# Windowed attention with a Mish MLP on one core: two key blocks merged by a predicated copy before the exponential

## Chip, cores and metric

The kernel runs on one core of one Trainium2 chip. The metric is the device time of one execution in microseconds (us); less is better. TensorE (PE), VectorE (DVE), ScalarE (ACT), GpSimd (POOL) and SyncE (SP, which issues the DMAs) each work through a queue of their own in order, and wait for one another through semaphores.

## What is computed

```python
def _attn_ref(q, k, v):                       # (8, 8, 576, 64) each
    scores = q @ k^T / sqrt(64)
    rel = pos[:, None] - pos[None, :]
    bias = slope[h] * -abs(rel)
    mask = (rel >= 0) & (rel < 128)
    attn = softmax(where(mask, scores + bias, -1e9))
    return attn @ v
def _moe_ref(x, w_in, w_out):                 # x (4608, 512), d_ff 2048
    h = x @ w_in
    g = h * tanh(softplus(h))                 # Mish
    return g @ w_out
```

A query sees itself and the 127 keys before it. With queries in blocks of 128, row r of a block sees the keys n <= r of its own block and the keys n > r of the block before: 128 keys in all, one for each column n.

## The kernel before

**Work.** There are 8 batches of 8 heads; heads go in pairs (4 pairs, `p`), and each pair has three units: `unit(b, p, 0)` (half 0: query blocks 0 and 1), `unit(b, p, 1)` (half 1: blocks 2 and 3) and `last_unit(b, p)` (the 64 queries that are left of 576; both heads in one tile). A unit is a list of steps: `scores` (PE, into a PSUM tile `s` of two banks, of which there are two), `peak` (DVE adds the bias table `nb`, finds the row's extreme `mx` and writes the scores to `pz`), `exps` (ACT, the sum goes to `sm`), `fold`, `scale`, `weights` (PE transposes the attention weights back into `s`, DVE copies them out), `values` (PE, into `o`), and `split_hi`/`split_lo` (ACT and DVE write the result as a high and a low float32r part, `x`).

**Two key blocks.** `peak` and `exps` work on 256 columns for each query block (128 for block 0, which has no block before it): the older key block and the own one, masked by the bias table. In batches 1 to 7 `fold` then adds the two halves of `pz` on GpSimd, so that 128 columns are left, `scale` multiplies by the reciprocal sums on DVE (lines 241-244), `weights` makes four transposes, and one DVE product with `masks` spreads them over two key blocks again (lines 263-268). In batch 0 nothing is folded: GpSimd scales 256 columns a block (lines 232-240), PE makes 6 or 8 transposes and DVE copies them (lines 249-259). The last queries' scores go into the unused columns of half 0's `s` tile in batches 1 to 7 (line 328), into a tile `w` in batch 0.

**MLP.** `first(c, j)` makes `h` (PE, 24 products of 512 columns, three for each of the four pairs' x and each half of `j`), 8 of them a batch; `h` shares the two buffers of `s`, and ACT's Mish empties one. `parts` splits g (ACT `gs`, GpSimd `gs`); `second` makes `po` in groups of six products. Weights arrive as 64-bit values and pass `sign_w` (ACT), `bits_w` (two DVE instructions, `ti`/`to`), `high_w` (ACT, `si`/`so`) and `low_w` (DVE).

**What sets the order.** Every instruction is recorded in program order (all appear under line 30). The program order is a sort of steps by hand-written times: batch 0 and the weights from `START`, `UNIT`, `X0`, `signs` and `bits` (lines 511-535); then, for each batch c, its `first` steps, followed by its `second` steps with the attention of batch c+1 laid between them at `4 * s + 0.8` (line 558). The numbers beside the steps (lines 303-315, 390-396) are those times.

Of the kernel before, what the change touches and what calls it, by code (L numbers as in the profile page):

```python
# [16 lines left out]
P = 128  # L17
# [20 lines left out]
def attention_mish_mlp(  # L38
# [69 lines left out]
    nl = const.tile([P, NP, 192], BF16, tag="nl", name="nl")  # L108
# [11 lines left out]
    make_upper_triangular(nc, masks[:, 1, :])  # L120
    xs = dram.tile([NCC, P, CH], F32, tag="xs", name="xs")
# [48 lines left out]
    def unit(b, p, half):  # L170
# [10 lines left out]
        def scores():  # L181
            qk = qkv[(b, p)]
            if b == 0 and (2 * p + half) % 3 == 2:
                s_ = [ps.tile([P, 512], F32, tag=f"po{i}", name=f"s{name}_{i}") for i in range(2)]
            else:
                t = ps.tile([P, 2, 512], F32, tag="s", name=f"s{name}", bufs=2)
                s_ = [t[:, i, :] for i in range(2)]
                if half == 0:
                    qkv[("s", b, p)] = t[:, :, :96]
            st["s"] = s_  # L190
            q0 = 0 if half == 0 else 832
            for a, j in enumerate(blocks):
                n = 256 if j else P
                for i in range(2):
                    pe.matmul(
                        s_[i][:, 256 * (a + 1) - n : 256 * (a + 1)], lhsT=qk[HEAD[i], q0 + a * P : q0 + (a + 1) * P],
                        rhs=qk[HEAD[i], 256 + (j + 1) * P - n : 256 + (j + 1) * P], start=True, stop=True,
                    )

        def peak(a):  # L200
            if a == 0:
                st["mx"] = at.tile([P, 4], F32, tag="mx", name=f"mx{name}")
                st["sm"] = at.tile([P, 4], F32, tag="sm", name=f"sm{name}")
                st["pz"] = at.tile([P, 4, 256], F32, tag="pz", name=f"pz{name}")
            mx, pz = st["mx"], st["pz"]
            n = 256 if blocks[a] else P
            for c in (a, a + 2):
                dve.tensor_tensor_reduce(
                    out=pz[:, c, :n], in0=st["s"][c // 2][:, 256 * (a + 1) - n : 256 * (a + 1)],
                    in1=nb[:, p, c // 2, 256 - n :], scale=-SCALE, scalar=3.0e38,  # L210
                    op0=ALU.add, op1=ALU.min, accum_out=mx[:, c : c + 1],
                )
# [10 lines left out]
        def fold():  # L223
            sm, pz = st["sm"], st["pz"]
            if b:
                two = pz if half else pz[:, 1:4:2]
                pool.tensor_tensor(out=two[:, :, :P], in0=two[:, :, :P], in1=two[:, :, P:], op=ALU.add)
            dve.tensor_scalar(out=sm, in0=sm, scalar1=1e-9, scalar2=None, op0=ALU.add)
            dve.reciprocal(sm, sm)

        def scale():
            if b == 0:
                for a, j in enumerate(blocks):
                    n = 256 if j else P
                    pool.tensor_tensor(
                        out=st["pz"][:, a::2, :n], in0=st["pz"][:, a::2, :n],
                        in1=st["sm"][:, a::2].rearrange("p (c n) -> p c n", n=1).to_broadcast([P, 2, n]),
                        op=ALU.mult,
                    )
                return  # L240
            dve.tensor_tensor(
                out=st["pz"][:, :, :P], in0=st["pz"][:, :, :P],
                in1=st["sm"].rearrange("p (c n) -> p c n", n=1).to_broadcast([P, 4, P]), op=ALU.mult,
            )

        def weights():
            pz = st["pz"]

            if b == 0:
                pf = st["pf"] = ff.tile([P, 2, 512], F32, tag="g", name=f"pf{name}", bufs=3)  # L250
                first = 0 if half else P
                for i in range(2):
                    for a, j in enumerate(blocks):
                        for u in range(2 if j else 1):
                            d = 256 * a + P * u if j else P
                            pe.transpose(st["s"][i][:, d : d + P], pz[:, 2 * i + a, u * P : (u + 1) * P], ident)
                for i in range(2):
                    dve.tensor_copy(pf[:, i, first:], st["s"][i][:, first:])
                return
# [3 lines left out]
            dve.tensor_tensor(  # L263
                out=pz.rearrange("p c (u n) -> p u c n", u=2),
# [4 lines left out]

# [33 lines left out]
        if b == 0:  # L303
            return [
                (0, scores), (0.1, lambda: peak(0)), (0.1, lambda: exps(0)), (0.15, lambda: peak(1)),
                (0.15, lambda: exps(1)), (0.5, fold), (0.55, scale),
                (1.6, weights), (2.25, values), (2.38, split_hi),
                (2.9 if p + 1 < NP else 2.4, split_lo),
# [3 lines left out]
            (0, scores), (0.02 + t, lambda: peak(0)), (0.025 + t, lambda: peak(1)),  # L312
            (0.026 + 27 * t, lambda: exps(0)), (0.026 + 27 * t, lambda: exps(1)), (0.27 + 33 * t, fold),
# [3 lines left out]
    def last_unit(b, p):  # L317
# [4 lines left out]
        def scores():  # L322
            qk = qkv[(b, p)]
            if b == 0:
                st["t"] = ps.tile([P, 512], F32, tag="w", name=f"pt{name}")
                st["s"] = st["t"][:, 256:448].rearrange("p (a n) -> p a n", a=2)
            else:
                st["s"] = qkv[("s", b, p)]
            for i in range(2):
                pe.matmul(  # L330
                    st["s"][:, i, :], lhsT=qk[:, 1152:1280], rhs=qk[:, 640 + 96 * i : 736 + 96 * i],
                    start=True, stop=True,
                )

        def peak():
            mx = st["mx"] = at.tile([P, 1], F32, tag="mxl", name=f"mx{name}")
            sm = st["sm"] = at.tile([P, 1], F32, tag="sml", name=f"sm{name}")
            pz = st["pz"] = at.tile([P, 192], F32, tag="pzl", name=f"pz{name}")
            dve.tensor_tensor_reduce(
                out=pz.rearrange("p (a n) -> p a n", a=2), in0=st["s"],  # L340
                in1=nl[:, p, :].rearrange("p (a n) -> p a n", a=2), scale=-SCALE, scalar=3.0e38,
# [3 lines left out]
        def exps():  # L345
            act.activation(st["pz"], st["pz"], AF.Exp, bias=st["mx"], scale=-1.0, accum_out=st["sm"])

        def fold():
            sm, pz = st["sm"], st["pz"]
            dve.tensor_scalar(out=sm, in0=sm, scalar1=1e-9, scalar2=None, op0=ALU.add)  # L350
            dve.reciprocal(sm, sm)
            if b == 0:
                pool.tensor_scalar(out=pz, in0=pz, scalar1=sm, scalar2=None, op0=ALU.mult)
                return
            dve.tensor_tensor(out=pz[:, :64], in0=pz[:, :64], in1=pz[:, P:], op=ALU.add)
            dve.tensor_scalar(out=pz[:, :P], in0=pz[:, :P], scalar1=sm, scalar2=None, op0=ALU.mult)
# [20 lines left out]
        def values():  # L377
            va = qkv[("v", b, p)]
            o = st["t"][:, P : P + LEFT]
            for n in range(2):  # L380
                k = 64 if n and b == 0 else P
                for i in range(2):
                    pe.matmul(
                        o[HEAD[i]], lhsT=va[:k, 3 + n, HEAD[i]], rhs=st["pf"][:k, n, i, :],
                        start=(n == 0), stop=(n == 1), skip_group_check=True,
                    )
            xo = at.tile([P, LEFT], F32, tag="xo", name=f"xo{name}", bufs=4)
# [6 lines left out]
        if b == 0:  # L394
            return [(0.28, scores), (0.3, peak), (0.3, exps), (1.3, fold), (1.65, weights), (2.12, values)]
        return [
            (0.01, scores), (0.04, peak), (0.31, exps), (0.5, fold), (1.54, weights), (1.995, values),
# [33 lines left out]
    def first(c, j):  # L431
        h = ps.tile([P, 2, CH], F32, tag="s", name=f"h{c}_{j}", bufs=2)
        split = NCC - 1 if c and j == 0 else NCC
# [78 lines left out]
    X0 = START + 9.45 * UNIT  # L512
# [133 lines left out]
```

## Time and profile before

| what | value |
|---|---|
| median of 3 runs | 1023.83 us (1023.41 to 1024.63) |
| the profiled execution's own time | 1023.82 us |
| its span in the trace | 1022.1 us |
| mean granted TensorE clock | 0.992 of full speed |
| busy shares PE, DVE, ACT, POOL | 96%, 42%, 37%, 26% |
| chain that ended last | PE 76%, DVE 12%, ACT 9%, issue 2% |

The busy share of PE says how much of the span some matmul was under way; what counts are the gaps, and the releaser named beside each. Times in the rows are microseconds from the span's start.

### The profile page before, as it was taken

To read this page: it belongs to the slowest core of one execution; us is meant where nothing else is said; L and a number is where in the kernel's file an instruction comes from. 1 tells how busy PE (TensorE), PEld (TensorE's weight loads), DVE (VectorE), ACT (ScalarE), POOL (GpSimd) and SP (SyncE) were. 2 spreads that over 40 slices of the span, in tenths; PEclk is the share of its full clock that TensorE was granted. 3 is DMA by queue.
4 is the path that set the end of the run, shared out by engine and by line. 5 is a ranking of instruction groups with operands and counts; after the bars stand their busy time and mean duration, and the time that the engine had idled before them with its cause. 6 is when DMAs were issued, how large, how long until landed. Compare 5 with 4: busy or idle time off the path is not lost.

```text
span 1022.1 us, 13726 instructions
## 1 busy us (share of the span) xinstructions
PE 979.1 (96%) x5308; PEld 790.9 (77%) x5308; DVE 425.3 (42%) x1118; ACT 377.8 (37%) x898; POOL 261.0 (26%) x230
## 2 busy tenths in 40 slices
PE   7799889999999999999999999999999999999998
PEld 4588668877788778877788778877887778888886
DVE  5797874046700763057502671077404770010000
ACT  4875533244323433245324342253324432331221
POOL 4310431033301531045103340144104330241043
PEclk8999999999999999999999999999999999999999
DMA  9930112003110121012200121021200201010001
GB/s 370 419 134 27 41 61 75 1 26 98 44 35 15 52 78 59 1 39 89 75 1 27 63 80 35 1 66 62 75 1 26 76 4 41 1 42 21 1 6 36
DMA packets 23392, 61.37 MB, mean 60 GB/s; under 512 B 6688, under 2 KB 7840, under 8 KB 21280
## 3 DMA queue, kind: packets, MB, share of 16 engines
q1 hardware_dynamic: 22096, 59.78, 17.2%
q8 instruction: 42, 0.69, 0.3%
q10 hardware_dynamic: 1232, 0.72, 0.2%
q14 instruction: 22, 0.18, 0.1%
HBM read 50.00 MB, written 10.49 MB: 59 GB/s over the span
## 4 chain that ended last, share of the span: by engine, by line
PE 76%; DVE 12%; ACT 9%; issue 2%; DMA 0%; POOL 0%; DVEq 0%; POOLq 0%; ACTq 0%
PE h L30 38%; PE po L30 22%; PE s L30 9%; ACT pz L30 7%; PE o L30 5%; DVE pz L30 5%; DVE pz_1l L30 1%; DVE pz_2l L30 1%; DVE pz_0l L30 1%; ACT gs L30 1%; DVE sm L30 1%; PE pt_0l L30 0%; PE pt_1l L30 0%; DVE pf L30 0%; PE pt_3l L30 0%
## 5 line engine op out<-in xcount | busy, mean ns | idle before, releaser
L30 PE MATMUL po<-so,gs 128*128 128x512 f32 x1728 | 411.8, 394 | 1.5 <-ACT gs L30 1.1
L30 PE MATMUL h<-x,si 128*128 128x512 f32 x1728 | 394.5, 390 | 1.2 <-DVE si L30 1.2
L30 PEld LDWEIGHTS h<-x,si 128*128 128x128 f32 x1728 | 323.7, 188 | 69.2 <-DVE si L30 1.7
L30 PEld LDWEIGHTS po<-so,gs 128*128 128x128 f32 x1728 | 321.7, 189 | 67.8 <-ACT gs L30 1.5
L30 POOL TENSOR_TENSOR gs<-g,gs 128x512 fp32r<-128x512 f32 x144 | 186.6, 1300 | 568.4 <-ACT gs L30 545.5
L30 DVE CUSTOM_DVE_ANT_0 pz<-s,nb 128x256 f32<-128x256 f32 (+1 forms) x256 | 82.6, 386 | 310.7 <-PE s L30 310.0
L30 ACT ACTIVATE g<-h 128x1024 f32<-128x1024 f32 x72 | 74.0, 1028 | 273.1 <-PE h L30 273.1
L30 ACT ACTIVATE pz<-pz,mx 128x256 f32<-128x256 f32 (+1 forms) x256 | 119.9, 470 | 70.4 <-DVE mx L30 70.4
L30 ACT ACTIVATE gs<-g 128x512 fp32r<-128x512 f32 x144 | 88.7, 624 | 127.1 <-PE po L30 127.1
L30 POOL TENSOR_TENSOR pz<-pz 128x256 f32<-128x256 f32 (+1 forms) x56 | 57.4, 1024 | 158.1 <-ACT pz L30 158.1
L30 PE MATMUL s<-qk 64*128 64x256 f32 (+2 forms) x624 | 77.8, 360 | 3.8 <-DMA qk<-in_qk_dram 3.8
L30 DVE TENSOR_TENSOR pz<-pz,sm 128x512 f32<-128x512 f32 x56 | 78.9, 1409 | 5.8
L30 PEld LDWEIGHTS s<-qk 64*128 64x128 f32 (+1 forms) x624 | 57.1, 192 | 21.2 <-issue 12.8
L30 DVE TENSOR_TENSOR pz<-s,masks 128x1024 f32<-128x1024 f32 x56 | 65.7, 1212 | 8.0 <-PE s L30 7.9
L30 PE MATMUL s<-ident,pz 128*128 128x128 f32 x280 | 43.6, 289 | 25.1 <-DVE pz L30 23.9
L30 PEld LDWEIGHTS s<-ident,pz 128*128 128x128 f32 x280 | 33.9, 148 | 34.9 <-issue 29.2
L30 DVE COPY ob<-po 128x512 f32<-128x512 f32 x18 | 12.3, 682 | 114.3 <-PE po L30 114.3
L30 ACT ACTIVATE x<-o 128x512 fp32r<-128x512 f32 x32 | 19.0, 594 | 95.0 <-PE o L30 95.0
L30 PE MATMUL o<-pz,va 128*64 128x128 f32 (+1 forms) x560 | 48.7, 320 | 0.0
L30 ACT ACTIVATION_READ_ACCUMULATOR pz<-pz,mx 128x1 f32 x256 | 48.0, 187 | 0.0
L30 PEld LDWEIGHTS o<-pz,va 128*64 128x64 f32 x560 | 33.9, 136 | 18.0 <-issue 7.4
L30 ACT ACTIVATE ob<-po 128x512 f32<-128x512 f32 x18 | 10.7, 596 | 51.4 <-PE po L30 51.4
(120 smaller groups left out, 388.6 us busy)
## 6 DMA issues: line engine op xcount, KB each, us to landing
qk<-in_qk_dram SPq DMA_DIRECT2D x31, 640.0 KB, 4.4
va<-in_v_dram SPq DMA_DIRECT2D x28, 320.0 KB, 3.3
wi<-in_moe_w_in_dram SPq DMA_DIRECT2D x8, 1024.0 KB, 14.3
wo<-in_moe_w_out_dram SPq DMA_DIRECT2D x8, 1024.0 KB, 20.4
out_dram<-ob SPq DMA_DIRECT2D x32, 256.0 KB, 2.0
qk<-in_v_dram SPq DMA_DIRECT2D x4, 320.0 KB, 6.3
xr<-xs SPq DMA_DIRECT2D x4, 256.0 KB, 2.8
out_dram<-ob SPq DMA_DIRECT2D x8, 128.0 KB, 2.3
```

The source lines that it names most:

```text
L30: ins = method(*args, **kwargs)
```

## The change

- The two key blocks are merged ahead of the exponential. A mask `older` (GpSimd builds it at the start) drives a DVE `copy_predicated` that overwrites, in PSUM, the own block's score by the older block's where n > r. `peak` then has 128 columns for every block, with a bias table to match, `exps` has 128 columns, and the fold is gone. The last queries get the same.
- `scale` moves to GpSimd for all batches (for the last queries in batch 0 alone); `sums` keeps the two small DVE instructions of `fold`.
- Batch 0 uses the way of the other batches: four transposes and one product with `masks`.
- The last queries' scores always get a tile of their own (`w`, in batch 0 `po1` for odd pairs); `values` is split, with `keep` writing the result out.
- The written times of batch 0 and of the weights are new; `first(0, 0)` takes the last pair's x behind the other three; the first Mish is placed at 3.2 instead of 0.3 behind its slot.

```diff
-    nl = const.tile([P, NP, 192], BF16, tag="nl", name="nl")
+    nl = const.tile([P, NP, P], BF16, tag="nl", name="nl")
...
+    older = const.tile([P, 192], BF16, tag="older", name="older")
+    make_upper_triangular(nc, older[:, :P], diag=False)
+    for i in range(2):
+        make_lower_triangular(nc, older[i * D : (i + 1) * D, P:])
+    older = older.bitcast(mybir.dt.uint16)
...
-            if b == 0 and (2 * p + half) % 3 == 2:
-                s_ = [ps.tile([P, 512], F32, tag=f"po{i}", name=f"s{name}_{i}") for i in range(2)]
...
+            t = ps.tile([P, 2, 512], F32, tag="s", name=f"s{name}", bufs=2)
+            st["s"] = [t[:, i, :] for i in range(2)]
+            st["all"] = t.rearrange("p i (c u n) -> p (i c) u n", u=2, n=P)
...
+        def peak():
...
+            v = st["all"] if half else st["all"][:, 1::2]
+            n = v.shape[1]
+            dve.copy_predicated(
+                v[:, :, 1], older[:, :P].rearrange("p (c n) -> p c n", c=1).to_broadcast([P, n, P]), v[:, :, 0]
+            )
+            for a, j in enumerate(blocks):
+                for i in range(2):
+                    dve.tensor_tensor_reduce(
+                        out=pz[:, 2 * i + a, :P], in0=st["s"][i][:, 256 * a + P : 256 * a + 256],
...
+            for c in (0, 2, 1, 3):
                 act.activation(
-                    pz[:, c, :n], pz[:, c, :n], AF.Exp, bias=mx[:, c : c + 1], scale=-1.0,
+                    st["pz"][:, c, :P], st["pz"][:, c, :P], AF.Exp, bias=st["mx"][:, c : c + 1], scale=-1.0,
...
-                pool.tensor_tensor(out=two[:, :, :P], in0=two[:, :, :P], in1=two[:, :, P:], op=ALU.add)
...
-            dve.tensor_tensor(
+            pool.tensor_tensor(
                 out=st["pz"][:, :, :P], in0=st["pz"][:, :, :P],
                 in1=st["sm"].rearrange("p (c n) -> p c n", n=1).to_broadcast([P, 4, P]), op=ALU.mult,
...
+            pf = st["pf"] = ff.tile([P, 4, 256], F32, tag="g", name=f"pf{name}", bufs=3) if b == 0 else pz
...
-                (0, scores), (0.1, lambda: peak(0)), (0.1, lambda: exps(0)), (0.15, lambda: peak(1)),
-                (0.15, lambda: exps(1)), (0.5, fold), (0.55, scale),
-                (1.6, weights), (2.25, values), (2.38, split_hi),
-                (2.9 if p + 1 < NP else 2.4, split_lo),
+                (-0.38 if p or half else 0, scores), (0.1, peak), (0.15, exps), (0.6, sums), (0.62, scale),
+                (1.3, weights), (1.75, values), (2.2 if p + 1 < NP else 1.85, split_hi),
+                ({NP - 2: 3.4, NP - 1: 1.98}.get(p, 2.62), split_lo),
...
-                st["s"] = qkv[("s", b, p)]
...
+            t = st["t"] = ps.tile([P, 512], F32, tag="po1" if b == 0 and p % 2 else "w", name=f"pt{name}")
...
+            dve.copy_predicated(older_[:, :64], older[:, P:], newer)
...
-    X0 = START + 9.45 * UNIT
+    X0 = START + 9.0 * UNIT
...
+    signs = [START + UNIT * t for t in (3.25, 4.25, 5.25, 6.25, 7.2, 7.5, 7.72, 8.2)]
+    signs += [X0 + t for t in (0.9, 1.9, 2.9, 3.9, 5.9, 8.4)]
...
-        steps.append((t + SLOT + 0.3, lambda j=j: mish[j]()))
+        steps.append((t + SLOT + (0.3 if j else 3.2), lambda j=j: mish[j]()))
```

**How the order moves.** In the rows below a tile's name ends in pair, half and a number, or in pair and `l` for the last queries.

DVE in batch 1, pair 2, from the last queries' scores to the masks, before:

```order
L30 RECIPROCAL sm_2_0_1199<-sm_2_0_1199 128x4
L30 TENSOR_TENSOR pz_2_0_1200<-pz_2_0_1200,sm_2_0_1199 128x4x128
L30 TENSOR_SCALAR sm_2l<-sm_2l 128x1
L30 RECIPROCAL sm_2l<-sm_2l 128x1
L30 TENSOR_TENSOR pz_2l<-pz_2l 128x64
L30 TENSOR_SCALAR pz_2l<-pz_2l,sm_2l 128x128
L30 TENSOR_SCALAR sm_2_1_1210<-sm_2_1_1210 128x4
L30 RECIPROCAL sm_2_1_1210<-sm_2_1_1210 128x4
L30 TENSOR_TENSOR pz_2_1_1211<-pz_2_1_1211,sm_2_1_1210 128x4x128
L30 TENSOR_TENSOR pz_2_0_1200<-s_2_0_1181,masks 128x2x4x128
L30 TENSOR_TENSOR pz_2_1_1211<-s_2_1_1186,masks 128x2x4x128
L30 TENSOR_TENSOR pf_2l<-pt_2l,masks 128x256
```

The same stretch with the change:

```order
L30 RECIPROCAL sm_2_0_1177<-sm_2_0_1177 128x4
L30 TENSOR_SCALAR sm_2l<-sm_2l 128x1
L30 RECIPROCAL sm_2l<-sm_2l 128x1
L30 TENSOR_SCALAR pz_2l<-pz_2l,sm_2l 128x128
L30 TENSOR_SCALAR sm_2_1_1205<-sm_2_1_1205 128x4
L30 RECIPROCAL sm_2_1_1205<-sm_2_1_1205 128x4
L30 TENSOR_TENSOR pz_2_0_1171<-s_2_0_1152,masks 128x2x4x128
L30 TENSOR_TENSOR pz_2_1_1183<-s_2_1_1157,masks 128x2x4x128
L30 TENSOR_TENSOR pf_2l<-pt_2l,masks 128x256
```

The two 512-column products by `sm` and the 64-column sum are gone from DVE; the small instructions on the sums stand close together.

GpSimd in the same pair, before:

```order
L30 TENSOR_TENSOR gs_1_2_1153<-g_1_659,gs_1_2_1153 128x512
L30 TENSOR_TENSOR pz_2_0_1200<-pz_2_0_1200 128x2x128
L30 TENSOR_TENSOR gs_1_3_1230<-g_1_659,gs_1_3_1230 128x512
L30 TENSOR_TENSOR pz_2_1_1211<-pz_2_1_1211 128x4x128
L30 TENSOR_TENSOR gs_1_4_1259<-g_2_739,gs_1_4_1259 128x512
```

With the change:

```order
L30 TENSOR_TENSOR gs_1_2_1124<-g_1_627,gs_1_2_1124 128x512
L30 TENSOR_TENSOR gs_1_3_1202<-g_1_627,gs_1_3_1202 128x512
L30 TENSOR_TENSOR pz_2_0_1171<-pz_2_0_1171,sm_2_0_1177 128x4x128
L30 TENSOR_TENSOR pz_2_1_1183<-pz_2_1_1183,sm_2_1_1205 128x4x128
L30 TENSOR_TENSOR gs_1_4_1231<-g_2_704,gs_1_4_1231 128x512
```

The two folds became two scalings, and `gs` of part 3 stands ahead of both instead of between them.

ACT around the first Mish (`g` from `h`), before:

```order
L30 ACTIVATE si_554<-ti_541 128x1024
L30 ACTIVATE x_3_556<-o_3_521 128x512
L30 ACTIVATE wo_127<-wo_127 128x1024
L30 ACTIVATE wo_129<-wo_129 128x1024
L30 ACTIVATE wo_131<-wo_131 128x1024
L30 ACTIVATE wo_133<-wo_133 128x1024
L30 ACTIVATE wo_135<-wo_135 128x1024
L30 ACTIVATE si_594<-ti_587 128x1024
L30 ACT_TABLE_LOAD
L30 ACTIVATE g_0_584<-h_0_559 128x1024
L30 ACTIVATE si_626<-ti_596 128x1024
L30 ACTIVATE si_632<-ti_628 128x1024
```

With the change:

```order
L30 ACTIVATE x_3_519<-o_3_492 128x512
L30 ACTIVATE si_525<-ti_522 128x1024
L30 ACTIVATE wo_134<-wo_134 128x1024
L30 ACTIVATE wo_136<-wo_136 128x1024
L30 ACTIVATE wo_138<-wo_138 128x1024
L30 ACTIVATE wo_140<-wo_140 128x1024
L30 ACTIVATE wo_142<-wo_142 128x1024
L30 ACTIVATE si_589<-ti_560 128x1024
L30 ACTIVATE wo_144<-wo_144 128x1024
L30 ACT_TABLE_LOAD
L30 ACTIVATE g_0_553<-h_0_528 128x1024
L30 ACTIVATE si_597<-ti_591 128x1024
```

One pass on `wo` more stands behind `si` of the second weight block and ahead of the first Mish, and the last pair's `x` now stands ahead of that `si`.

## Rows read from the trace of the kernel before

**Rows 1.** The waits of PE over the span (us in total, times, longest)

```profile
PE s L30 <- DVE pz L30: 23.9, 21, 3.1
```

**Rows 2.** Timeline of PE in batch 2, pair 0: start, duration, instruction, [idle before]

```profile
225.81 0.60 PE L30 MATMUL s<-ident,pz 128*128 128x128 f32 x4
227.38 0.63 PE L30 MATMUL s<-ident,pz 128*128 128x128 f32 x4 [0.97 <-DVE pz L30]
...
230.80 1.74 PE L30 MATMUL o<-pz,va 128*64 128x256 f32 x20
...
232.70 2.40 PE L30 MATMUL s<-qk 64*128 64x128 f32 x20
```

**Rows 3.** Timeline of DVE in the same stretch

```profile
217.78 0.29 DVE L30 CUSTOM_DVE_ANT_0 pz<-s,nb 128x128 f32<-128x128 f32 x1 [46.34 <-PE s L30]
...
217.99 0.28 DVE L30 CUSTOM_DVE_ANT_0 pz<-s,nb 128x128 f32<-128x128 f32 x1
...
225.58 1.66 DVE L30 TENSOR_TENSOR pz<-pz,sm 128x512 f32<-128x512 f32 x1
227.16 2.34 DVE L30 TENSOR_TENSOR pz<-s,masks 128x1024 f32<-128x1024 f32 x2
...
233.22 0.69 DVE L30 TENSOR_TENSOR x<-o,x 128x512 fp32r<-128x512 f32 x1 [0.17 <-ACT x L30]
```

**Rows 4.** The tile sm: ns least/median/most of each operation

```profile
L30 DVE TENSOR_TENSOR pz<-pz,sm x56: 692/1458/1716, 105.8 to 837.1; 128x512 f32<-128x512 f32 x56
```

**Rows 5.** Timeline of ACT, the same pair: an exponential of 128 columns

```profile
218.11 0.40 ACT L30 ACTIVATE pz<-pz,mx 128x128 f32<-128x128 f32 x1 [1.18 <-DVE mx L30]
```

**Rows 6.** Timeline of GpSimd, batch 0 to batch 2

```profile
40.55 2.04 POOL L30 TENSOR_TENSOR pz<-pz,sm 128x512 f32<-128x512 f32 x2 [0.46 <-ACT x L30]
62.52 4.01 POOL L30 TENSOR_TENSOR gs<-g,gs 128x512 fp32r<-128x512 f32 x2 [19.93 <-ACT gs L30]
```

**Rows 7.** Part 5 of the page: GpSimd on 512 columns, and a DVE copy out of PSUM

```profile
L30 POOL TENSOR_TENSOR gs<-g,gs 128x512 fp32r<-128x512 f32 x144 | 186.6, 1300 | 568.4 <-ACT gs L30 545.5
...
L30 DVE COPY ob<-po 128x512 f32<-128x512 f32 x18 | 12.3, 682 | 114.3 <-PE po L30 114.3
```

**Rows 8.** Timeline of PE from the first long run of products to batch 1, pair 1

```profile
50.08 43.40 PE L30 MATMUL h<-x,si 128*128 128x512 f32 x190 [1.25 <-DVE si L30]
...
105.12 1.20 PE L30 MATMUL po<-so,gs 128*128 128x512 f32 x4 [1.07 <-ACT gs L30]
...
111.06 1.09 PE L30 MATMUL s<-ident,pz 128*128 128x128 f32 x4 [3.14 <-DVE pz L30]
...
131.19 1.09 PE L30 MATMUL s<-ident,pz 128*128 128x128 f32 x4 [2.38 <-DVE pz L30]
```

**Rows 9.** Stretches of PE: length, busy time by engine, granted clock (behind POOL)

```profile
111.06:116.00 4.94, 4.94 (x19) 3.95 (x21) 4.37 (x5) 0.94 (x2) 1.64 (x2) 0.71 0.00 0
...
131.19:136.20 5.01, 5.01 (x19) 3.96 (x21) 3.04 (x4) 1.12 (x2) 0.09 (x1) 0.68 0.14 52
227.38:231.00 3.62, 3.62 (x19) 2.85 (x21) 2.45 (x3) 0.63 (x1) 0.68 (x1) 1.00 0.00 0
```

**Rows 10.** Timeline of DVE, batch 0 and the first weights

```profile
22.46 0.99 DVE L30 COPY pf<-s 128x384 f32<-128x384 f32 x2
...
40.29 0.99 DVE L30 COPY pf<-s 128x384 f32<-128x384 f32 x2
...
51.10 0.68 DVE L30 TENSOR_SCALAR ti<-wi 128x1024 uint32<-128x1024 uint32 x1
51.82 1.23 DVE L30 SCALAR_TENSOR_TENSOR ti<-wi,ti 128x1024 uint32<-128x1024 uint32 x1
```

**Rows 11.** Timeline of ACT around the first Mish

```profile
50.36 5.31 ACT L30 ACTIVATE wo<-wo 128x1024 f32<-128x1024 f32 x5
...
56.63 1.28 ACT L30 ACT_TABLE_LOAD   x1
57.92 1.03 ACT L30 ACTIVATE g<-h 128x1024 f32<-128x1024 f32 x1
```

More of the change, by code (lines that the diff above doesn't have):

```diff
@@ L195, in scores @@
                     pe.matmul(
-                        s_[i][:, 256 * (a + 1) - n : 256 * (a + 1)], lhsT=qk[HEAD[i], q0 + a * P : q0 + (a + 1) * P],
+                        st["s"][i][:, 256 * (a + 1) - n : 256 * (a + 1)], lhsT=qk[HEAD[i], q0 + a * P : q0 + (a + 1) * P],
                         rhs=qk[HEAD[i], 256 + (j + 1) * P - n : 256 + (j + 1) * P], start=True, stop=True,
                     )
[L200 to L212, printed above, removed]
@@ L218, in exps, with sums @@
+        def exps():
+            sm = st["sm"] = at.tile([P, 4], F32, tag="sm", name=f"sm{name}")
+            for c in (0, 2, 1, 3):
                 act.activation(
-                    pz[:, c, :n], pz[:, c, :n], AF.Exp, bias=mx[:, c : c + 1], scale=-1.0,
+                    st["pz"][:, c, :P], st["pz"][:, c, :P], AF.Exp, bias=st["mx"][:, c : c + 1], scale=-1.0,
                     accum_out=sm[:, c : c + 1],
                 )
[L223 to L226, printed above, removed]
-                pool.tensor_tensor(out=two[:, :, :P], in0=two[:, :, :P], in1=two[:, :, P:], op=ALU.add)
+        def sums():
+            sm = st["sm"]
@@ L247, in weights @@
             pz = st["pz"]
[L249 to L259, printed above, removed]
             pt = st["s"][0].rearrange("p (c n) -> p c n", c=4)
@@ L311, in unit @@
         return [
[L312 to L313 removed]
+            (0, scores), (0.02 + t, peak), (0.026 + 27 * t, exps), (0.27 + 33 * t, sums),
             (0.33 + 33 * t, scale), (1.53, weights), (1.99, values), (2.02, split_hi), (2.02, split_lo),
@@ L323, in scores @@
             qk = qkv[(b, p)]
[L324 to L327, printed above, removed]
-                st["s"] = qkv[("s", b, p)]
[L329 to L333, printed above, removed]
+            t = st["t"] = ps.tile([P, 512], F32, tag="po1" if b == 0 and p % 2 else "w", name=f"pt{name}")
+            st["s"] = [t[:, 256:384], t[:, 384:448]]
+            for s_, k in zip(st["s"], (slice(640, 768), slice(768, 832))):
+                pe.matmul(s_, lhsT=qk[:, 1152:1280], rhs=qk[:, k], start=True, stop=True)
         def peak():
             mx = st["mx"] = at.tile([P, 1], F32, tag="mxl", name=f"mx{name}")
-            sm = st["sm"] = at.tile([P, 1], F32, tag="sml", name=f"sm{name}")
-            pz = st["pz"] = at.tile([P, 192], F32, tag="pzl", name=f"pz{name}")
+            pz = st["pz"] = at.tile([P, P], F32, tag="pzl", name=f"pz{name}")
+            older_, newer = st["s"]
+            dve.copy_predicated(older_[:, :64], older[:, P:], newer)
             dve.tensor_tensor_reduce(
-                out=pz.rearrange("p (a n) -> p a n", a=2), in0=st["s"],
-                in1=nl[:, p, :].rearrange("p (a n) -> p a n", a=2), scale=-SCALE, scalar=3.0e38,
+                out=pz, in0=older_, in1=nl[:, p, :], scale=-SCALE, scalar=3.0e38,
                 op0=ALU.add, op1=ALU.min, accum_out=mx,
@@ L394, in last_unit @@
         if b == 0:
-            return [(0.28, scores), (0.3, peak), (0.3, exps), (1.3, fold), (1.65, weights), (2.12, values)]
+            return [
+                (0.55, scores), (0.65, peak), (0.75, exps), (1.15, sums), (1.16, scale), (1.615, weights), (1.76, values),
+                (2.19, keep),
+            ]
         return [
-            (0.01, scores), (0.04, peak), (0.31, exps), (0.5, fold), (1.54, weights), (1.995, values),
+            (0.01, scores), (0.04, peak), (0.31, exps), (0.5, sums), (0.5, scale), (1.54, weights), (1.995, values), (1.996, keep),
         ]
```

79 lines of the change are left out of this document (30 added, 49 removed).

## Prediction

> **What bounds the kernel now.** I read the busy shares first: PE 96%, no other engine above 42%. So the time is PE's work plus the gaps between its instructions, and the next view is what PE waits for. One line carries nearly all of it: PE waits 21 times, 23.9 us in total and 3.1 at most, for DVE's `pz` before it can go on with `s` [rows 1]. The timelines of one pair show what that is. PE transposes half 0's weights (225.81), then stands still for 0.97 us until half 1's are scaled (227.38) [rows 2]. DVE starts that scaling at 225.58 and needs 1.66 us [rows 3]; nothing on PE can be put ahead of it, as PE's order is fixed. The first two of these gaps, in batch 1, are 3.14 and 2.38 us [rows 8]; the other 19 share 23.9 - 5.5 = 18.4 us, 0.97 each: three pairs in each of the batches 1 to 7, as a batch's last pair has none. The clock belongs to it: behind the two long gaps the granted clock is 0.71 over 4.94 us and 0.68 over 5.01 us, a mix of the levels 1.2 and 2.4 GHz, while behind a gap of 0.97 us it is 1.00 [rows 9]. That costs another 4.94 x 0.29 = 1.4 and 5.01 x 0.32 = 1.6 us. Up to the first long run of MLP products, at 50.08 [rows 8], DVE, PE, ACT and GpSimd take turns.
>
> **Batches 1 to 7: the weights of half 1.** The two products on DVE (0.69 us at best, 1.46 in the median [rows 4]) leave DVE. GpSimd pays two scalings in place of two folds. I price each at 1.3 us, the mean of its work on 512 columns [rows 7]; the ends are 1.02 us (half of 2.04) and 2.0 us (half of 4.01) [rows 6]. The exponential has 128 columns everywhere, 0.40 us [rows 5]; the score passes have 128 columns, one every 0.21 us (217.78 to 217.99) [rows 3].
>
> The predicated copy is in no row. The nearest is DVE's copy of 512 columns out of PSUM, 0.68 us [rows 7]; I take 0.68 for half 1 (512 columns) and 0.34 for half 0. The ends are half of it (nothing excludes a faster pass) and 1.72 us, the longest DVE instruction on 512 columns [rows 4].
>
> Now the order, counted from S, the end of a pair's 20 score products. Before, the first score pass starts at S, 217.78 [rows 3], though half 0's products are done earlier: the last queries' scores, the last of the 20, are in the same tile. With a tile of their own, half 0 can start when DVE has finished the pair before. Its last instruction there ends at 233.22 + 0.69 = 233.91, S being 232.70 + 2.40 = 235.10 [rows 2, 3], so at S - 1.2. The queues then run:
> - DVE: copy 0.34 and four passes 0.84, to S + 0.0; copy 0.68 and four passes, to S + 1.5; the last queries' 0.4, to S + 1.9.
> - ACT: half 0's four exponentials end at S + 1.1, one `gs` later half 1 runs from S + 1.7 to S + 3.3, the last queries to S + 3.7.
> - GpSimd: `gs` to S + 3.0, the scaling of half 0 to S + 4.3. Half 1's waits for the sums, behind two small instructions and the last queries' scaling on DVE: S + 4.9 to S + 6.2.
>
> PE asks for half 0 at 225.81 = S + 8.0 and for half 1 0.6 us later, at S + 8.6 [rows 2, 3]. So half 1 is 2.4 us early, where it was 0.97 late. At the upper end of the copy (1.72) it is 1.5 x 1.04 = 1.6 us later, and still early. What is late next is `values`: DVE's two products with the masks (2.34 us [rows 3]) and the last queries' 0.4 end at 225.81 + 0.6 + 2.7 = 229.1; PE wants them 3.4 us (227.38 to 230.80 [rows 2]) after the second transposes, now at 229.8. That is 0.7 us of cover. The scores of the next pair need a free tile for the last queries; DVE copies the old one out while PE is still at the 16 other products, so no wait.
>
> Gain: 19 x 0.97 = **18.4 us**. In batch 1 the second gap (2.38) lies in the same steady order, with one weight pass of 1.2 us on DVE between the halves, within the 2.4 us of cover: 2.38 + 1.6 - 0.1 = **3.9 us** with its clock. The first gap is another matter. DVE is held there by the weights (`wo` behind the first batch's last Mish and a table load, the same order with the change), so GpSimd's `gs` and both scalings come late: PE gets half 0 about 0.8 and half 1 about 1.3 us late, behind the wait of 1.07 us for `gs` [rows 8] that stays. I take 1.0 of the 3.14 and half of the 1.4 for the clock: **1.7 us**. Ends: 0 and 4.5.
>
> **Batch 0 and the first Mish.** A pair takes (40.29 - 22.46) / 2 = 8.9 us between copies of `pf` [rows 10]. Gone: 6 of 14 transposes (0.15 us each, [rows 2]: 0.9 on PE) and half of GpSimd's 2.04 us for half 1 [rows 6]. Added: 1.0 us of predicated copies on DVE. The copies of `pf` and the masks cost the same. The chain DVE, PE, GpSimd walked through for a pair gives 8.45; its ends are 7.9 (the copies beside other work) and 9.9 (only they count). The first pair is some 1.5 us earlier, the fourth's `pf` so 2.4. After that the first product needs one weight block instead of two: the second block's bits (0.68 + 1.23 us [rows 10]) now stand behind. So the first products start near 45, not 50.08.
>
> This is given back at the third `h`. `h` has two buffers, and the first must be emptied by Mish. In ACT's new order there stand, behind the second block's `si`, five passes on `wo` (5.31 us), one more `si` and `wo` (1.0 each), the table load (1.28) and Mish (1.03) [rows 11]: 10.5 us from the end of that block's bits, which is 3.1 to 3.8 us after PE's first product. PE fills two `h` in 48 x 43.40 / 190 = 11.0 us [rows 8]. It waits 2.6 to 3.3 us, long enough for the clock to fall as behind the gaps of batch 1, another 1.5. So 5 earlier, minus 3.0 and 1.5, minus some half-clock products ahead: **0**, between -3 and +4.
>
> **Sum.** 18.4 + 3.9 + 1.7 + 0 = 24.0 us off. The profiled execution took 1023.82 us (span 1022.1), the median is 1023.83, so both give **999.8 us**. A difference under 0.2%, 2 us, could not be told from none.
>
> **Rivals.**
> - *The start keeps its gain.* The third `h` waits little or the clock holds. For it: the wait is a difference of two sums of some 11 us. Against: the order puts Mish behind all those passes. 3.0 + 1.5 more: 995.3 us. Chance 0.13.
> - *GpSimd gets in the way.* DVE's product by `sm` is 0.69 us alone and mostly 1.46 [rows 4], GpSimd's `gs` 1.3 and up to 2.0 [rows 6, 7]: the two hold each other up. With 2.0 us for `gs` and both scalings, and 0.7 us in which DVE's small sums wait for GpSimd to end, half 1 is ready at S + 9.0, 0.4 us late: 20 x 0.4 = 8 back, 1002 to 1008, 1005 in the middle. Against: only `gs` and the first scaling can run while the sums wait, since the second stands behind them. The Trainium skill, "Perfetto Trace Analysis", section "Optimizing Scalar/DVE Operations", says that GpSimd and DVE share a read port, so that moving work between them might not help; by that rule this is the likely case. The trace agrees that they hold each other up, but not that there is no room. Chance 0.10.
> - *The wait moves to `values`.* If DVE's masks come 1.7 us late, PE waits 1.0 us there instead: 19 us stay, 1019. Against: the 0.7 us of cover, on a DVE that has lost two products. Chance 0.04.
> - *The predicated copy is slow.* At y us for 512 columns half 1 is ready at S + 5.2 + 1.5 y, and batch 0 pays 4 x 1.5 (y - 0.68). Gain and loss meet at y = 2.7; at 3.0 it is 20 x 1.1 + 14 = 36 more, 1036 us, slower than before. For it: no row shows it, and it reads and writes PSUM. Against: 2.7 is four times the copy's row and over the longest row on 512 columns, 1.72. Chance 0.04.
>
> **Numbers.** The forecast has 0.69; its own range is 997 to 1003. With the first rival below and most of the second above, the range is 994.5 to 1006 and leaves out some 0.12. All cases but the slow copy are faster by more than 0.2%: 0.95 faster, 0.01 no difference, 0.04 slower.
>
> **What would show it.** Right: PE's line of waits for DVE's `pz` gone or under 2 us and no line of that size for GpSimd's `pz`; the second half's transposes right behind the first's; clock 1.00 in batch 1's second pair; a wait of `h` for ACT's `g` near 3 us around 56; the predicated copies at 0.68 and 0.34. Wrong: a wait of `s` for GpSimd's `pz` in every pair, a wait of `o` for the masks, a copy beyond 1.7 us, or a first `h` that starts later than 48.

## Result and profile after

The changed kernel takes 995.31 us in the median of four runs (994.80 to 995.78); before, on the same chip, 1024.23 (1023.41 to 1024.63). The ratio is 0.9719, with a 95% interval of 0.9702 to 0.9735. The forecast was 999.8 with a range from 994.5: the time lies in the range, at its lower end. The profiled execution took 994.80 us, its span is 993.1, so 29.0 us less than the span before.

The waits of PE after the change (us in total, times, longest):

```profile
PE s L30 <- DMA qk<-in_qk_dram: 3.7, 1, 3.7
PE s L30 <- POOL pz L30: 3.2, 4, 1.2
PE s L30 <- DVE pf L30: 2.8, 3, 1.0
PE o L30 <- DVE pf L30: 2.3, 1, 2.3
PE h L30 <- ACT g L30: 2.2, 1, 2.2
PE po L30 <- ACT gs L30: 1.3, 1, 1.3
```

The line of [rows 1], 23.9 us for DVE's `pz`, is gone, and no line of that size has come for GpSimd. What is left stands in batch 0 and in batch 1's first pair. A steady pair, timeline of PE in batch 2, to be held against [rows 2]:

```profile
249.86 1.04 PE L30 MATMUL s<-ident,pz 128*128 128x128 f32 x8
...
250.76 3.02 PE L30 MATMUL po<-so,gs 128*128 128x512 f32 x12
253.71 1.74 PE L30 MATMUL o<-pz,va 128*64 128x256 f32 x20
```

Both halves' transposes are now one run of eight without a gap. The timeline of GpSimd in the same pair (compare [rows 6, 7]) shows why:

```profile
244.00 1.30 POOL L30 TENSOR_TENSOR gs<-g,gs 128x512 fp32r<-128x512 f32 x1 [5.33 <-ACT gs L30]
245.26 1.04 POOL L30 TENSOR_TENSOR pz<-pz,sm 128x512 f32<-128x512 f32 x1
247.00 1.04 POOL L30 TENSOR_TENSOR pz<-pz,sm 128x512 f32<-128x512 f32 x1 [0.70 <-DVE sm L30]
```

Half 1's scaling ends at 248.04. PE asks for half 1 after four transposes, at 249.86 + 0.52 = 250.38: 2.3 us of cover, where the forecast had 2.4. In a batch's first pair it is 1.5 us, since ACT loads its table ahead of the exponentials there.

The predicated copies, from the groups of DVE by form (busy us, mean ns of one):

```profile
L30 DVE COPY_PREDICATED s<-older,s 128x512 f32<-128x512 uint16 x32 | 22.1, 692 | 1.4 <-PE s L30 1.4
...
L30 DVE COPY_PREDICATED s<-older,s 128x256 f32<-128x256 uint16 x32 | 13.5, 422 | 276.3 <-PE s L30 276.3
```

512 columns take 0.69 us (forecast 0.68, the copy of [rows 7]); 256 take 0.42 (forecast 0.34). The timeline of PE from the first MLP products to batch 1's second pair, to be held against [rows 8]:

```profile
44.45 11.79 PE L30 MATMUL h<-x,si 128*128 128x512 f32 x48
58.43 34.53 PE L30 MATMUL h<-x,si 128*128 128x512 f32 x144 [2.19 <-ACT g L30]
...
104.84 1.20 PE L30 MATMUL po<-so,gs 128*128 128x512 f32 x4 [1.33 <-ACT gs L30]
...
107.56 0.66 PE L30 MATMUL s<-ident,pz 128*128 128x128 f32 x4 [0.63 <-POOL pz L30]
109.12 0.66 PE L30 MATMUL s<-ident,pz 128*128 128x128 f32 x4 [0.90 <-POOL pz L30]
...
124.97 1.04 PE L30 MATMUL s<-ident,pz 128*128 128x128 f32 x8
```

The long run of products starts at 44.45 instead of 50.08 (before, two of the 192 stood ahead of it, at 48.09), but ends at 92.96 instead of 93.48. In between the third `h` waits 2.19 us for Mish, and then the granted clock falls. Stretches of PE with the clock in the last column but two (compare [rows 9]):

```profile
60.00:70.00 10.00, 10.00 (x40) 8.16 (x39) 9.79 (x9) 5.37 (x7) 4.18 (x2) 0.86 0.00 0
...
109.12:114.10 4.98, 4.98 (x37) 3.90 (x39) 4.61 (x5) 0.64 (x1) 3.72 (x3) 1.00 0.01 2
126.00:130.00 4.00, 4.00 (x30) 2.99 (x30) 2.45 (x3) 1.12 (x2) 2.13 (x2) 1.00 0.36 135
```

0.86 is a mix of the levels 1.2 and 2.4 GHz: the 144 products take 34.53 us where they take 32.94 at full clock (as in experiments 7 and 8), 1.6 us more. The third row lies in batch 1's second pair: the clock is whole there, where it was 0.68. Mish came late because of what stands ahead of it on ACT, as the order said ([rows 11] before):

```profile
48.74 5.31 ACT L30 ACTIVATE wo<-wo 128x1024 f32<-128x1024 f32 x5
53.91 1.09 ACT L30 ACTIVATE si<-ti 128x1024 fp32r<-128x1024 f32 x1
54.85 1.18 ACT L30 ACTIVATE wo<-wo 128x1024 f32<-128x1024 f32 x1
56.06 1.28 ACT L30 ACT_TABLE_LOAD   x1
57.35 1.02 ACT L30 ACTIVATE g<-h 128x1024 f32<-128x1024 f32 x1
```

The 29.0 us, stage by stage, beside the terms of the forecast:

| stage | how it is read | measured | forecast |
|---|---|---|---|
| to the end of batch 0's `h` | 93.48 to 92.96 | 0.5 | 0 |
| batch 1, first pair, from there to its values | 22.34 to 19.63 | 2.7 | 1.7 |
| batch 1, second pair, values to values | 20.30 to 16.23 | 4.1 | 3.9 |
| 19 pairs | 17.37 to 16.23 each | 21.7 | 18.4 |
| sum | | 29.0 | 24.0 |

The first row is one execution against one. Experiments 4 and 5 leave batch 0 as it was, and their `h` ends at 93.89 and 91.10; experiment 10 repeats the change, and there it ends at 92.22. So the 0.5 can't be told from the spread between executions. In that repeat the pairs take the same to 0.1 us, but for batch 1's first, where the clock fell.

### The profile page after: what moved, and what is told of

Same layout as the page of the kernel before. It is cut to its first block, busy times and chain, and to the rows that moved or that the text cites. A ratio compares the mean times of both kernels' runs of the same rounds, so it can differ in the third digit from the quotient of the medians.

```text
span 993.1 us, 13627 instructions
## 1 busy us (share of the span) xinstructions
PE 967.3 (97%) x5280; PEld 785.1 (79%) x5280; DVE 323.6 (33%) x1118; ACT 358.9 (36%) x898; POOL 255.5 (26%) x228
## 4 chain that ended last, share of the span: by engine, by line
PE 92%; ACT 2%; DVE 2%; issue 0%; POOL 0%; ACTq 0%; DVEq 0%; POOLq 0%
PE po L30 39%; PE h L30 39%; PE s L30 7%; PE o L30 5%; PE pt_2l L30 1%; PE pt_1l L30 1%; PE pt_3l L30 1%; ACT wo L30 1%; PE pt_0l L30 1%; DVE ti L30 0%; ACT si L30 0%; ACT pz L30 0%; DVE to L30 0%; ACT L30 0%; DVE pf L30 0%
## 5 line engine op out<-in xcount | busy, mean ns | idle before, releaser
L30 DVE COPY_PREDICATED s<-older,s 128x256 f32<-128x256 uint16 x64 | 35.6, 557 | 277.6 <-PE s L30 277.6
L30 ACT ACTIVATE pz<-pz,mx 128x128 f32<-128x128 f32 x256 | 99.3, 389 | 46.5 <-DVE mx L30 44.2
L30 POOL TENSOR_TENSOR pz<-pz,sm 128x512 f32<-128x512 f32 x64 | 66.5, 1039 | 38.8 <-DVE sm L30 22.8
L30 PE MATMUL s<-qk 64*128 64x256 f32 (+1 forms) x512 | 60.7, 375 | 6.5 <-DMA qk<-in_qk_dram 3.7
L30 DVE CUSTOM_DVE_ANT_0 pz<-s,nb 128x128 f32<-128x128 f32 x256 | 59.1, 287 | 2.8
L30 PEld LDWEIGHTS s<-qk 64*128 64x128 f32 x512 | 42.5, 193 | 14.3 <-DVE pf L30 3.8
L30 PE MATMUL s<-ident,pz 128*128 128x128 f32 x256 | 34.5, 274 | 3.2 <-POOL pz L30 3.2
L30 PEld LDWEIGHTS s<-ident,pz 128*128 128x128 f32 x256 | 29.4, 141 | 8.9 <-POOL pz L30 4.7
```

What stands on the lines that cost most here:

```text
L30: ins = method(*args, **kwargs)
```

## Experiments

Two theories were put against each other. **Cover**: the gap is a matter of when half 1's weights are ready, and whatever makes them ready before PE asks removes it whole, whichever engine scales. **GpSimd**: the moved scaling is what counts, for good or ill. Each group of experiments ran on one chip, beside the kernel before: it took 1020.97 us with 1 to 4, 1021.29 with 5 and 6, 1022.04 with 7 and 8, 1022.07 with 9 and 10. Experiments 1 to 6 are one execution each, so a microsecond or two between them says nothing by itself; the gaps in their traces do. No experiment leaves out any of the computation.

**1. The change with the scaling on DVE** (batches 1 to 7):

```diff
-            pool.tensor_tensor(
+            (dve if b else pool).tensor_tensor(
                 out=st["pz"][:, :, :P], in0=st["pz"][:, :, :P],
```

> The changed kernel with the scaling of batches 1 to 7 back on DVE; merge and separate tile stay. Cover theory (the weights of half 1 were 0.97 us late and now have about 2 us of cover, to which all parts of the change add): DVE's product, 0.7 to 1.7 us, ends near S + 5 to S + 6.5, still before PE asks at S + 8.6, so no wait of s for pz in the pairs of batches 2 to 7 and a time within 2 us of 995.3. GpSimd theory (the wait went because DVE and GpSimd no longer hold each other up over the scaling): waits of about 1 us come back in three pairs a batch, 1015 us or more.

Measured 994.28 us, 0.974 of before on that chip; the change has 0.972 and, in run 10, 0.974. A pair takes 16.23 us (233.43 to 249.66) with either. So the move to GpSimd gives nothing here that can be told, and costs nothing. Yet GpSimd's work does hold DVE's up. Timelines of PE (first fence), DVE (second) and GpSimd (third) in batch 2 of this run:

```profile
249.66 1.03 PE L30 MATMUL s<-ident,pz 128*128 128x128 f32 x8
```

```profile
246.69 1.70 DVE L30 TENSOR_TENSOR pz<-pz,sm 128x512 f32<-128x512 f32 x1
```

```profile
246.55 1.29 POOL L30 TENSOR_TENSOR gs<-g,gs 128x512 fp32r<-128x512 f32 x1 [1.45 <-ACT gs L30]
```

The product takes 1.70 us beside `gs`, where it takes 0.69 alone [rows 4]; `gs` takes 1.29, no more than its mean of 1.30 [rows 7]. The product still ends at 248.39, 1.8 us before PE asks for half 1 (at 249.66 + 0.52 = 250.18). The Trainium skill, "Perfetto Trace Analysis", section "Optimizing Scalar/DVE Operations", says that the two share a read port and that moving work between them might not help. The trace agrees: 1.70 against 0.69, and the same time for the kernel. In the kernel before, where half 1 was late, the same move did help (experiment 4). The loss that the second rival made of it (1005 us) did not come.

**2. The change with the last queries' scores back in half 0's tile** (batches 1 to 7):

```diff
-            t = st["t"] = ps.tile([P, 512], F32, tag="po1" if b == 0 and p % 2 else "w", name=f"pt{name}")
-            st["s"] = [t[:, 256:384], t[:, 384:448]]
+            if b == 0:
+                t = st["t"] = ps.tile([P, 512], F32, tag="po1" if p % 2 else "w", name=f"pt{name}")
+                st["s"] = [t[:, 256:384], t[:, 384:448]]
+            else:
+                st["s"] = [qkv[("s", b, p)][:, 0, :P], qkv[("s", b, p)][:, 1, :64]]
```

> The changed kernel with the last queries' scores of batches 1 to 7 back in the unused columns of half 0's tile. Cover theory: the first predicated copy starts 1.3 us later, half 1's cover falls from 2.3 to about 1.0 us (0.2 in a batch's first pair), no wait, time within 2 us of 995.3. Rival (the tile is what removed the wait): waits of about 1 us in three pairs a batch, 1015 us or more.

Measured 995.64 us, and 16.23 us a pair (233.95 to 250.18), with no gap in the transposes: the tile is not needed either.

**3. Both undone**, so that the merge (with batch 0's new order) stands alone; the edit is that of 1 and 2 together.

> The changed kernel with both undone: scaling on DVE and last scores in half 0's tile; only the merge (128 columns, no fold) is left in batches 1 to 7. Cover theory: half 1 ready near S + 6.5 to S + 7.8, before S + 8.6; waits none or below 0.3 us, 995 to 1001 us. Rival (the merge alone is not enough): waits of 0.5 us and more in three pairs a batch, 1007 us or more.

Measured 994.59 us, 16.23 us a pair (233.71 to 249.94). Timeline of PE in batch 2:

```profile
249.94 1.03 PE L30 MATMUL s<-ident,pz 128*128 128x128 f32 x8
```

The merge alone is enough. Which part of it counts, the fold that is gone or the 128 columns instead of 256 on DVE and ACT, was not separated. DVE's product by `sm` takes 0.705 us in the mean there (56 of them, 39.5 us), half of what it took before [rows 4], since here it falls between two `gs` of GpSimd; what falls beside them now is the scaling of the last queries, 1.27 us in pair 2 where it takes 0.29 in experiment 1.

**4. The kernel before, with only the scaling moved to GpSimd:**

```diff
-            dve.tensor_tensor(
+            pool.tensor_tensor(
                 out=st["pz"][:, :, :P], in0=st["pz"][:, :, :P],
```

> The kernel before with nothing changed but the scaling of batches 1 to 7 moved to GpSimd, behind the folds that stay there. Cover theory: GpSimd does fold, part, scaling, fold, scaling by S + 7.7, 0.9 us before PE asks: the 0.97 us waits go and with them 19 x 1.16 us and some of the two long gaps, 998 to 1004 us. Rival (GpSimd has no room for four passes a pair): waits of s for GpSimd's pz in their place, 1015 to 1030 us.

Measured 1009.59 us, 11.4 less than before on that chip: between the two numbers. The timelines of PE (first fence) and GpSimd (second) in batch 2, first pair and the one behind it, tell why:

```profile
222.30 0.60 PE L30 MATMUL s<-ident,pz 128*128 128x128 f32 x4
224.05 0.66 PE L30 MATMUL s<-ident,pz 128*128 128x128 f32 x4 [1.15 <-POOL pz L30]
...
239.90 1.13 PE L30 MATMUL s<-ident,pz 128*128 128x128 f32 x8
```

```profile
219.82 1.04 POOL L30 TENSOR_TENSOR pz<-pz,sm 128x512 f32<-128x512 f32 x1
220.82 1.29 POOL L30 TENSOR_TENSOR pz<-pz 128x512 f32<-128x512 f32 x1
222.96 1.04 POOL L30 TENSOR_TENSOR pz<-pz,sm 128x512 f32<-128x512 f32 x1 [0.84 <-DVE sm L30]
```

GpSimd now folds and scales. In the first pair of each of the batches 2 to 7, where the table load makes everything later, that is 1.15 us too late; in the other pairs it is just in time. So 13 of the 19 gaps are gone, and such a pair takes 16.32 us (239.90 to 256.22) instead of 17.39 (243.18 to 260.57 before). From the `values` of batch 1's second pair to the end that makes 11.7 us (885.98 to 874.33): 13 gaps give 13.9, and the six gaps that are left, 1.15 instead of 0.97, and the batches' last pairs take some 2 back. Batch 1's second pair gives another 3.0, its gap being 0.85 instead of 2.38, and the start is 0.5 longer: 14.2 us between the spans (1022.1 and 1007.9). It is a question of cover, pair by pair.

**5. The kernel before, with only a tile of their own for the last queries' scores:**

```diff
-            if b == 0:
-                st["t"] = ps.tile([P, 512], F32, tag="w", name=f"pt{name}")
-                st["s"] = st["t"][:, 256:448].rearrange("p (a n) -> p a n", a=2)
-            else:
-                st["s"] = qkv[("s", b, p)]
+            st["t"] = ps.tile([P, 512], F32, tag="w", name=f"pt{name}")
+            st["s"] = st["t"][:, 256:448].rearrange("p (a n) -> p a n", a=2)
```

> The kernel before with nothing changed but a tile of their own for the last queries' scores in batches 1 to 7. Half 0's score passes can start 1.2 us earlier. Cover theory: the chain moves with them and half 1, 0.97 us late before, is just in time: waits of 0 to 0.4 us, 1000 to 1010 us. Rival (the chain hangs on DVE and GpSimd holding each other up, not on its start): waits stay at 0.7 to 1.0 us, 1018 to 1024 us.

Measured 998.09 us, 23.2 less than before on that chip, and more than was expected. Half 0 no longer waits for the last of the 20 score products, and that is enough for every pair but batch 1's first two. Timeline of PE in batch 1:

```profile
108.67 1.09 PE L30 MATMUL s<-ident,pz 128*128 128x128 f32 x4 [3.13 <-DVE pz L30]
...
128.88 0.63 PE L30 MATMUL s<-ident,pz 128*128 128x128 f32 x4 [0.97 <-DVE pz L30]
...
144.68 1.04 PE L30 MATMUL s<-ident,pz 128*128 128x128 f32 x8
```

A pair takes 16.22 us there, 22.0 us less than before from the `values` of batch 1's second pair to the end (885.98 to 864.01), much as with the change. So each of two parts of the change removes the 19 gaps by itself; together they only add cover.

**6. The change with GpSimd made late**: idle products of 256 columns ahead of half 1's scaling, two in one kernel, five in the other.

```diff
         def scale():
+            if b and half:
+                for _ in range(2):
+                    pool.tensor_tensor(out=idle, in0=idle, in1=idle, op=ALU.mult)
             pool.tensor_tensor(
```

> The changed kernel with two idle GpSimd products of 256 columns (0.74 us each, on a scratch tile) ahead of half 1's scaling in batches 1 to 7: half 1 is 1.5 us later. Cover theory (2.3 us in pairs 1 and 2, 1.5 in a batch's first pair): no wait in pairs 1 and 2, up to 0.2 us in first pairs, within 3 us of 995.3. Rival (the cover is smaller than the rows say, or GpSimd's later parts become the wait): 1003 us or more.

> The same with five idle products: half 1 is 3.7 us later, past the cover. Cover theory: a wait of s for GpSimd's pz of about 1.4 us in pairs 1, 2 and 3 and 2.2 us in first pairs, each costing 0.2 us more than the idle time that the profile lists; 28 x about 1.8 = 50 us with the idle time alone, 1035 to 1060 us with the clock falling behind some. Rival (a gap costs only its idle time): the difference to the changed kernel equals the listed idle time.

Measured 997.02 and 1017.13 us. With two, the pairs still take 16.23 us, and no gap comes back but in batch 1's first pair (1.69 in place of 0.90). With five, every pair has its gap again, but a small one: 0.22 us, and 1.03 in the first pairs of batches 2 to 7, whose cover was 1.5. Timelines of PE and GpSimd with five, batch 2:

```profile
242.44 0.60 PE L30 MATMUL s<-ident,pz 128*128 128x128 f32 x4
243.25 0.66 PE L30 MATMUL s<-ident,pz 128*128 128x128 f32 x4 [0.22 <-POOL pz L30]
...
259.08 0.60 PE L30 MATMUL s<-ident,pz 128*128 128x128 f32 x4
259.90 0.66 PE L30 MATMUL s<-ident,pz 128*128 128x128 f32 x4 [0.22 <-POOL pz L30]
```

```profile
255.47 3.37 POOL L30 TENSOR_TENSOR idle<-idle 128x256 f32<-128x256 f32 x5
258.80 1.04 POOL L30 TENSOR_TENSOR pz<-pz,sm 128x512 f32<-128x512 f32 x1
```

The time is below the 1035 us that were expected. The mechanism is as forecast, the size was my arithmetic: the five take 3.37 us, and 0.70 of it falls into the time in which GpSimd waited for the sums anyway. So half 1 is 2.67 us later against 2.3 us of cover. The run also prices a gap: a pair takes 259.08 - 242.44 = 16.64 us, 0.41 more than 16.23, for 0.22 us that the timeline lists as idle.

**7. The change with the weights' sign passes (`sign_w`) around the first Mish moved**: two of the last six go ahead of the second weight block's `si` on ACT, where it was idle for 2.62 us, and the other four stand behind it without a break:

```diff
-    signs += [X0 + t for t in (0.9, 1.9, 2.9, 3.9, 5.9, 8.4)]
+    signs += [START + UNIT * 8.9, START + UNIT * 8.9] + [X0 + t for t in (0.9, 1.9, 2.9, 3.9)]
```

> The changed kernel with two of the six sign passes on w_out moved ahead of the second weight block's high part on ACT, where ACT sat idle for 2.6 us, and the sixth directly behind the fifth. The passes ahead of the first Mish theory: Mish comes 2.1 us earlier, the third h waits 0 to 0.3 us instead of 2.19, the clock does not fall behind it (1.6 us): 3.5 us less, 991.3 to 992.5 us. Rival (another wait takes its place, the weight block's low part or DVE): 994 us or more.

Measured 994.6 us in the median (991.51 to 996.01, four runs), ratio 0.9719 (0.9699 to 0.974): by this it can't be told from the change, and it misses the 991.3 to 992.5 that were expected. The profiled execution (span 991.8) shows both what came and what went. Timeline of PE:

```profile
57.13 32.94 PE L30 MATMUL h<-x,si 128*128 128x512 f32 x144 [0.87 <-ACT g L30]
...
106.25 0.78 PE L30 MATMUL s<-ident,pz 128*128 128x128 f32 x4 [0.90 <-POOL pz L30]
...
106.89 4.47 PE L30 MATMUL po<-so,gs 128*128 128x512 f32 x12
```

The wait of the third `h` is 0.87 us (with 0.36 ahead of it for `si`), the clock stays whole, and `h` ends at 90.07 instead of 92.96. But in batch 1's first pair, with the same gaps as in the change, the clock now falls behind the second: twelve products take 4.47 us instead of 3.02. That gives back 1.5 of the 2.9 us. For the other three executions the record has the mean granted clock: 0.997 at 991.51 us, 0.993 at 995.70 and 0.992 at 996.01, with 0.994 at 993.51 for the profiled one. So in these four the time goes with the clock; where it fell in them, no profile here shows.

**8. The same, and the last-but-one weight block's passes behind its sign pass (three on DVE, the high part on ACT) moved behind the score passes of batch 1's first pair:**

```diff
-((-0.2, 0.2, 0.4, 0.7), (2.3, 8.4, 8.5, 8.9))
+((-0.2, 1.2, 2.35, 4.0), (2.3, 8.4, 8.5, 8.9))
```

> The same, and the two DVE passes, the high and the low part of the seventh w_out block moved behind the score passes of batch 1's first pair. The waits of 1.33, 0.63 and 0.90 us in that pair come from that block standing ahead of the scores on DVE: without it they are gone, some 3 us with the refills, 987.5 to 989.5 us. Rival (the late block makes PE wait at its own products, or the exponentials are late behind the table load): 990.5 us or more.

Measured 987.98 us (987.37 to 988.22, five runs), ratio 0.966 (0.9646 to 0.9674): this version beats both kernels. PE has no gap left in batch 1 (the first pair's eight transposes still take 1.30 us instead of 1.03, so its weights come just in time):

```profile
56.34 32.94 PE L30 MATMUL h<-x,si 128*128 128x512 f32 x144 [0.21 <-ACT g L30]
...
101.04 1.30 PE L30 MATMUL s<-ident,pz 128*128 128x128 f32 x8
...
117.52 1.03 PE L30 MATMUL s<-ident,pz 128*128 128x128 f32 x8
```

**9. The second of these edits alone, and 10. the change itself on the same chip.**

> The change with only the last-but-one weight block's two DVE steps moved behind batch 1's score passes. Theory: in batch 1's first pair the scores wait on DVE behind that block's passes (96.50 to 101.85), and this alone makes the wait of 1.33 for gs and the two of 0.63 and 0.90 for pz. In the run with both steps moved, 28.24 us went from the end of h to the transposes of pair 1, where the change takes 32.01: so 3.8 us less than the change, 991.0 to 992.0, with the wait of the third h still near 2.2. Rival: the whole gain of that run over the change came from the earlier passes on the weights ahead of the first Mish, and moving the last-but-one block gives nothing: 994.5 to 996.

> The changed kernel itself on the same chip, as the measure for the run above: 994.5 to 996, a granted clock of 1.00 between 100 and 110 us. If the clock falls there, as it did in the run with the earlier passes alone, it should show as some 1.5 us more between the end of h and the transposes of pair 1.

Measured 991.37 us (ratio 0.9691, 0.9677 to 0.9706) and 995.61 (0.9736, 0.9719 to 0.9754); the intervals don't meet. Timeline of PE in 9:

```profile
58.51 34.55 PE L30 MATMUL h<-x,si 128*128 128x512 f32 x144 [2.11 <-ACT g L30]
...
121.33 1.03 PE L30 MATMUL s<-ident,pz 128*128 128x128 f32 x8
```

With the edit alone, from the end of `h` (58.51 + 34.55 = 93.06) to the second pair's transposes (121.33) it takes 28.27 us instead of 32.01: 3.7, as expected, with the third `h` still waiting 2.11. So the first pair was held by that block: in the change DVE is at it from 96.50 to 101.85, with a wait of 1.19 us for its high part on ACT, and takes up the scores only then. The edit moves all of this, so the shares of DVE and ACT are not told apart. In 8, 3.7 us and, from the earlier end of `h`, 3.7 more make the 7.4 us between the spans 993.1 and 985.7. The medians say why both are needed: beside 995.61 us for the change, 7 alone gives 1.0 us, 9 alone 4.2, both 7.6. With 7 alone a part goes back to the clock behind the gaps of the first pair, and in 8 these gaps are gone.

The repeat of the change ends at the same time by another way. Timeline of PE:

```profile
59.24 32.98 PE L30 MATMUL h<-x,si 128*128 128x512 f32 x144 [1.87 <-ACT g L30]
...
109.17 4.33 PE L30 MATMUL po<-so,gs 128*128 128x512 f32 x12
```

Behind a wait of 1.87 us the clock did not fall this time; it fell in batch 1's first pair, and from the end of `h` to pair 1 it took 33.59 us instead of 32.01, the 1.5 that were named for that case.

## Why the prediction was right, and where it was off

- **The 19 gaps: right in kind, mis-sized.** The term was 0.97 us each, the listed idle. It is 1.14 from pair to pair. The rest is the broken run of transposes. Timeline of PE before, batch 2, second pair:

```profile
243.18 0.60 PE L30 MATMUL s<-ident,pz 128*128 128x128 f32 x4
...
245.24 3.02 PE L30 MATMUL po<-so,gs 128*128 128x512 f32 x12
```

From the first transpose to the next `po` product that is 2.06 us; after, 249.86 to 250.76 = 0.90. Eight in a run take 1.04 us, twice four take 0.60 + 0.63: 0.19 us go with the gap. Experiment 6 shows the same 0.19 (0.41 lost for 0.22 idle). 21.7 - 18.4 = 3.3 us are two thirds of the whole miss of 5.0.
- **Half 1's cover: right.** 2.4 forecast, 2.3 measured; experiment 6 shows its end where it should be. That the sum came out so near is partly two errors that cancel: half 1's scaling takes 1.04 us, not 1.3, but starts at S + 5.2 (247.00, with S at 241.10 + 0.66 = 241.76), not S + 4.9. Of this delay the larger predicated copies (0.42 and 0.69 for 0.34 and 0.68) are 0.1 us; ACT's idle 0.29 us ahead of its `gs` would make up the rest.
- **Which part does it: not asked, and it matters.** The prediction treated merge, tile and scaling as one. Experiments 3 and 5 show that the merge alone or the tile alone removes these gaps, and experiment 1 that the move to GpSimd then adds nothing that can be told. By itself it removes 13 of the 19 (experiment 4).
- **Batch 1's second pair: right**, 4.1 for 3.9: gap and clock both back.
- **Batch 1's first pair: mis-sized.** I took 1.0 of 3.14 and half of the clock's 1.4. The two waits for `pz` left are 0.63 and 0.90, 1.6 less than 3.14, and the clock stayed at 1.00 in this execution, so all of the 1.4 came back; 0.3 of the sum went the other way. Experiments 7 and 10 show that the clock does fall there in other executions, so half was no bad guess; the 0.6 us of the gap was the error. What holds the pair was named rightly (DVE behind the weight block), and experiment 9 shows it.
- **The start: right in each step.** Products near 45: 44.45. A wait of 2.6 to 3.3 us: 2.19, a little less than forecast. 1.5 us for the clock: 1.6. The half-clock products ahead, for which no number was given: the first 48 took 11.79 us, not 11.0, at a granted clock of 0.95. And the 5 us that were to be given back were counted from 50.08, though two products (0.5 us of work) lay ahead of that. So 5.6 - 0.5 - 0.8 - 2.2 - 1.6 leaves 0.5; forecast 0.
- **The rivals.** "The start keeps its gain" was priced at 995.3, which is the time that came; but it isn't what happened, since the third `h` waited and the clock fell. The missing 5 us came for the most part from the steady pairs and the first pair. So that the time lies in the range is partly luck: the forecast's own range was 997 to 1003, and the lower end of 994.5 was there for this rival, while the terms that were too small were others. GpSimd in the way, the wait at `values` and the slow copy did not come: PE waits for none of them in a steady pair.

## What to carry to other kernels

A gap between two pieces of a run on PE costs more than its listed idle; price it by the distance between the same points of two neighbouring periods, one with a gap and one without (a batch's last pair had none here). When an edit consists of several, ask of each how much earlier it makes the late operand, and compare that with the lateness: where each is enough, the others buy cover and no time. And look behind the gaps that remain for what stands on the late engine in front of the work: two moves of weight passes gave another 7 us.

## What the runs showed of the hardware

- A predicated copy inside PSUM costs as much as a plain copy out of it: 0.692 us for 512 columns (copy: 0.688), 0.422 for 256, 0.224 for 64.
- GpSimd multiplies 512 columns by four sums in 1.04 us, while two full operands of 512 columns take it 1.30 (the subtraction `gs`) and 1.29 (the sum in experiment 4's fold).
- Ahead of the third `h` PE waited 2.0 to 2.3 us in six of the profiled executions (the change, experiments 1, 2, 3, 9 and the second of 6), and the clock fell behind it in each; in four it waited 0.21, 0.87, 1.77 and 1.87 us (8, 7, the first of 6, 10), and the clock stayed whole.
- The same gap does not always cost the clock. In batch 1's first pair it stayed whole behind a gap of 0.90 us in one execution of the change, where it had fallen behind the third `h`, and fell behind the same 0.90 in another (10), where it had not. The times of the two differ by 0.8 us.
